# One pool of four PSUM banks for the spectral transforms and the down blocks, and filter tiles negated one step later

## The chip, the cores and the metric

The kernel runs on one core of a Trainium2 chip. Its time is device microseconds (us) of one execution; the median of three runs is given. A profile is one more execution, recorded by the hardware profiler. The engines are TensorE (PE; PEld are its weight loads), VectorE (DVE), ScalarE (ACT), GpSimd (POOL) and SyncE (SP), each with its own instruction list that it works off in order. PSUM is the accumulator memory that TensorE writes; it has eight banks of 128 x 512 fp32.

## The reference

```python
def _A_ref(x, w_r, w_i):                      # x: 1 x 2048 x 448
    X = rfft2(x, axes=(-2, -1)) * (w_r + 1j * w_i)
    return irfft2(X, s=(S, D), axes=(-2, -1))

def _B_ref(x, W_gate, W_up, W_down):          # 448 -> 1792 -> 448
    gate = x @ W_gate
    gate = gate * (gate > 0)
    return (gate * (x @ W_up)) @ W_down

xn = _layernorm(x, axis=-1)
return x + _A_ref(xn, w_r, w_i) + _B_ref(xn, W_gate, W_up, W_down)
```

So the output is the input plus a filter in the two-dimensional spectrum of the layer-normed input plus a gated MLP of the same normed input.

## The kernel before, in words

Token rows are read as 16 tiles n2 of 128 x 448 and worked on in four chunks of four tiles (512 tokens). A normed chunk stands transposed in an SBUF tile T0 to T3, as a high and a low fp16 part, so that products of three fp16 matmuls give nearly fp32 accuracy. Three kinds of work share TensorE; every one of its matmuls after the opening has the helper line L499:

- *gate/up units* (`gu_unit`): for one of the 14 slices f of the hidden width and one chunk, 20 to 22 matmuls of 128x512 into a pair of PSUM banks called gu. ScalarE then takes the relu (L1061), VectorE multiplies it by the up half (L1065, the last reader of the pair), ScalarE and VectorE split the product into its two fp16 parts h (L1069, L1073).
- *down blocks*: for one tile n2 and one group of slices (`GROUPS`, 5, 5 and 4), 15 or 12 matmuls of 128x448 into one bank called dn. A block is seeded by ScalarE with the scaled running sum xy (`dn_seed`, L1090), and ScalarE writes the bank back to xy (`dn_post`, L1101). `dn_add` (L1108) is the other way: VectorE adds a bank that was not seeded to xy; only the last four blocks (`dn_end`) use it.
- *transforms*: the forward ones `f_dft` (48 matmuls of 64x58) and `f_sdft` (fp32, 64x464) and the inverse ones `i_sdft` and `i_ddft` (48 each). Each fills two PSUM banks, the two halves of one tile fx. ScalarE empties both halves in one instruction (`f_dft` L527, `f_y` L610, `i_part` L866) or in two (`i_ddft`, L909). `two_banks` (L507) writes one element of a fresh pair by ScalarE before the first matmul; VectorE folds what f_dft gave (L538 and on, tile eb), and f_sdft reads the folded tile. `row_dft` makes two small matmuls in one bank.

PSUM is divided by tile names: gu two pairs (four banks), dn two single banks, fx one pair. In the filter stage the half-filter tiles wf come by DMA, and `wneg` (L682) negates a part of each on ScalarE.

What sets the order: the first 45 us follow a handwritten list (`OPENING`). Behind it a list of gate/up units and down blocks is walked; with each unit a share of background steps (the list `bg`, with costs by which a unit takes as many as it has room for) is emitted: LayerNorm of later chunks, folds, transforms, filter, stores. A list scheduler then puts the instructions of each engine in an order, by readiness in its own model of the engines, by priority (`high_priority`) and by constraints (`issue_after`). A different number of banks therefore also changes which instruction it finds ready, and so the order on every engine.

## Time and profile before

| what | value |
|---|---|
| median of three runs | 445.41 us (445.02 to 445.5) |
| the profiled execution | 444.57 us |
| its span (first to last instruction) | 442.8 us |
| instructions in it | 8438 |
| TensorE busy | 429.2 us, 97% |
| VectorE busy | 376.6 us, 85% |
| ScalarE busy | 261.1 us, 59% |
| mean granted TensorE clock | 0.995 |
| waits of TensorE on L499 for a semaphore, longest | 3.5 us on L507 |

A group row of the profile gives line, engine, operation, what is written and read with its size, count, busy time in all, mean of one in ns, and the engine's idle time just before them with what ended it. A timeline row gives start, length and count, with idle time before it in brackets. A row of waits gives the sum, the number and the longest. The windows give the busy time of each engine in a stretch and the granted clock of TensorE, where 1.00 is full speed.

### The profile page before, as it was taken

The page shows a single profiled execution, that of the slowest core. Times are in us where ns is not written, and L with a number is a line of the kernel's source. Part 1 is how long each engine was busy: PE and PEld are TensorE (multiplying, and loading weights), DVE is VectorE, ACT ScalarE, POOL GpSimd, SP SyncE. Part 2 cuts the span into 40 slices and gives each one's busy share as a digit, 9 for nine tenths or more (in the row PEclk, how much of TensorE's full clock was granted, in tenths as well). Part 3 has the DMA queues.
Part 4 walks back from the last instruction along what each step waited for, and adds up shares of the span by engine and source line. Part 5 has one row for each costly group of instructions (what it writes and reads, how often), then busy time and mean ns, then how long its engine had stood idle before and what let it go on. Part 6 is the DMA issues. An engine that isn't in the chain of part 4 may idle for free.

```text
span 442.8 us, 8438 instructions
## 1 busy us (share of the span) xinstructions
PE 429.2 (97%) x3222; PEld 201.6 (46%) x3222; DVE 376.6 (85%) x804; ACT 261.1 (59%) x503; POOL 29.5 (7%) x72
## 2 busy tenths in 40 slices
PE   6999999699999999999999999999999999999995
PEld 2644544344444444444444444444454544544453
DVE  6898799999386999999999999599989869869533
ACT  6897484755645674754353562675766665755752
POOL 1140040310100110000000010010000000000000
PEclk9999999999999999999999999999999999999999
DMA  7769994230000731345404000021221021230112
GB/s 257 260 155 285 333 262 51 39 72 2 2 3 6 233 104 55 96 134 151 127 19 113 1 0 1 1 57 32 49 53 43 28 71 24 71 86 0 64 64 85
DMA packets 37721, 38.63 MB, mean 87 GB/s; under 512 B 18928, under 2 KB 33072, under 8 KB 37680
## 3 DMA queue, kind: packets, MB, share of 16 engines
q1 hardware_dynamic: 37680, 38.09, 30.5%
q8 instruction: 25, 0.41, 0.4%
q14 instruction: 16, 0.13, 0.1%
HBM read 23.20 MB, written 3.67 MB: 61 GB/s over the span
## 4 chain that ended last, share of the span: by engine, by line
PE 49%; DVE 31%; DMA 8%; ACT 4%; SPq 3%; issue 3%; POOL 1%; ACTq 0%; DVEq 0%; POOLq 0%
PE gu L499 27%; PE dn L499 15%; PE fx L499 5%; DMA wst<-in_wgu 3%; DMA y<-in_xr 3%; DVE g L1065 2%; SPq L724 2%; DVE h L1073 2%; DVE y L589 2%; DVE y L590 2%; DVE y L690 2%; DVE y L691 2%; DMA sw<-y 2%; DVE y L603 1%; DVE y L602 1%
## 5 line engine op out<-in xcount | busy, mean ns | idle before, releaser
L499 PE MATMUL gu<-T,wt 128*128 128x512 f16 (+2 forms) x1250 | 269.3, 377 | 0.5 <-DVE g L1065 0.5
L499 PEld LDWEIGHTS <-wt 128*128 128x128 f16 (+1 forms) x1250 | 111.2, 98 | 145.1 <-issue 25.2
L499 PE MATMUL dn<-wdt,h 128*128 128x448 f16 x624 | 127.7, 353 | 0.1
L499 PEld LDWEIGHTS <-h 128*128 128x128 f16 x624 | 59.5, 98 | 58.3 <-issue 2.2
L1069 ACT ACTIVATE h<-g 128x512 f16<-128x512 f32 x56 | 35.1, 627 | 57.5 <-DVE g L1065 57.4
L1061 ACT ACTIVATE g<-gu 128x512 f32<-128x512 f32 x56 | 33.0, 589 | 34.6 <-PE gu L499 34.5
L1065 DVE SCALAR_TENSOR_TENSOR g<-gu,g 128x512 f32<-128x512 f32 x56 | 38.3, 685 | 17.5 <-ACT g L1061 17.4
L1073 DVE TENSOR_TENSOR h<-g,h 128x512 f16<-128x512 f32 x56 | 38.3, 686 | 8.3 <-ACT h L1069 8.1
L1101 ACT ACTIVATE xy<-dn,dsc 128x448 f32<-128x448 f32 x44 | 27.4, 627 | 25.6 <-PE dn L499 25.3
L1090 ACT ACTIVATE dn<-xy,dinv 128x448 f32<-128x448 f32 x44 | 27.5, 629 | 0.4
L961 DVE SCALAR_TENSOR_TENSOR wt<-wst,wsc,wt 128x512 f16<-128x512 f32 x28 | 20.3, 745 | 4.6 <-ACT wt L957 4.6
L957 ACT ACTIVATE wt<-wst,wsc 128x512 f16<-128x512 f32 x28 | 19.0, 711 | 1.8 <-DVE wsc L244 1.8
L237 POOL PARTITION_ALL_REDUCE wm<-wm x15 | 7.7, 515 | 174.9 <-ACT junk L234 174.9
L234 ACT ACTIVATE junk<-wst 128x512 bf16<-128x512 f32 x28 | 17.4, 622 | 3.1 <-DMA wst<-in_wgu 2.9
L909 ACT ACTIVATE xy<-fx,fsc 128x448 f32<-128x448 f32 x16 | 9.3, 631 | 15.3 <-PE fx L499 15.3
L307 DVE BATCH_NORM_STATS2 bst<-y 128x6 f32<-128x448 f32 x16 | 9.2, 615 | 6.1 <-DMA y<-in_xr 6.1
L871 DVE TENSOR_TENSOR yu<-wf 128x512 f32<-128x512 f32 x8 | 5.5, 691 | 9.1 <-ACT wf L866 9.1
L590 DVE TENSOR_TENSOR y<-y 128x928 f32<-128x928 f32 (+1 forms) x11 | 11.8, 1077 | 0.3 <-DMA row<-y 0.2
L589 DVE TENSOR_TENSOR y<-y 128x928 f32<-128x928 f32 (+1 forms) x11 | 11.9, 1077 | 0.2
L866 ACT ACTIVATE wf<-fx 128x1024 f32<-128x1024 f32 x8 | 8.1, 1018 | 5.9 <-PE fx L499 5.9
L846 DVE SCALAR_TENSOR_TENSOR vt<-wst,fsc,vt 128x464 f16<-128x464 f32 x16 | 10.5, 697 | 0.5 <-ACT vt L841 0.4
L473 DVE TENSOR_TENSOR wst<-wst 128x116 f32<-128x116 f32 x48 | 10.5, 273 | 0.2
(157 smaller groups left out, 477.7 us busy)
## 6 DMA issues: line engine op xcount, KB each, us to landing
wst<-in_wgu SPq DMA_DIRECT2D x28, 256.0 KB, 4.6
wf<-in_wf SPq DMA_DIRECT2D x16, 232.0 KB, 2.8
sw<-y SPq DMA_DIRECT2D x64, 58.0 KB, 2.0
sw<-wst SPq DMA_DIRECT2D x32, 116.0 KB, 2.2
y<-in_xr SPq DMA_DIRECT2D x16, 224.0 KB, 4.8
xy<-in_x SPq DMA_DIRECT2D x16, 224.0 KB, 4.8
out<-xy SPq DMA_DIRECT2D x15, 224.0 KB, 2.0
wdst<-in_wd SPq DMA_DIRECT2D x14, 224.0 KB, 4.5
```

Of the source, the lines that this page charges most:

```text
L234: A.activation(mt([128, 512], BF16, "junk")[:, 0:src.shape[-1]], src, AF.Square, scale=SQ, accum_out=acc)
L499: r = P.matmul(*a, **k)
L589: V.tensor_tensor(t, a, b, op=OP.add)
L590: V.tensor_tensor(b, a, b, op=OP.subtract)
L957: A.activation(w[:, 0:4, :], wst[f, g], AF.Copy, scale=wsc[f, g])
L961: V.scalar_tensor_tensor(w[:, 4:8, :], st, sc, w[:, 0:4, :], op0=OP.mult, op1=OP.subtract)
L1061: last["A"] = A.activation(g1s[f, q], hps[f, q][:, 0, :], AF.Relu, scale=2.0 ** -22).ins
L1065: last["V"] = V.scalar_tensor_tensor(g1, hps[f, q][:, 1, :], 2.0 ** -22, g1, op0=OP.mult, op1=OP.mult).ins
L1069: A.activation(ht[f, q][:, 0, :], g1s[f, q], AF.Copy)
L1073: V.tensor_tensor(h[:, 1, :], g1s.pop((f, q)), h[:, 0, :], op=OP.subtract)
L1090: A.activation(dps[n2][:, 0:D], xy[n2], AF.Copy, scale=dinv[:, g:g + 1])
L1101: last["A"] = A.activation(xy[n2], dps[n2][:, 0:D], AF.Copy, scale=dsc[:, g:g + 1]).ins
```

## The change

Transforms, down blocks, `row_dft` and the end blocks take their banks from one pool of four single banks, name dn, in turn (`dn_bank`, `fx`). A transform takes two of them. An instruction that emptied both halves of a pair is now two, one for each bank (f_dft, f_y and i_part; 24 instructions become 48). The counter `banks` counts the banks taken after the opening, and blocks that get one of the first six are *bare*: they are not seeded, their first matmul starts the sum, and `dn_post` adds them by VectorE (`dn_add`) instead of by ScalarE; three blocks are. The two matmuls of row_dft are written so that the first covers 464 columns. And `wneg` moves from the end of the step before to the head of the step that multiplies by the tile.

```diff
--- before.py
+++ after.py
@@ -172,20 +172,11 @@
         return main.tile(shape, dt, name=name, bufs=bufs)
 
     def dn_bank():
-        return psum.tile([128, 512], F32, name="dn", bufs=2)
-
-    def fx2():
-        return psum.tile([128, 2, 512], F32, name="fx", bufs=1)
+        state["banks"] = state.get("banks", 0) + ("opened" in state)
+        return psum.tile([128, 512], F32, name="dn", bufs=4)
 
     def fx():
-
-        if "opened" in state:
-            return fx2()[:, 0]
-        if "fx" not in state:
-            state["fx"] = [fx2(), 1]
-        t = state["fx"]
-        t[1] = 1 - t[1]
-        return t[0][:, t[1]]
+        return dn_bank()
 
     xv = x.rearrange("(p n) d -> p n d", n=16)
     xrv = xr.rearrange("(p n) d -> p n d", n=16)
@@ -503,9 +494,9 @@
 
     def two_banks():
 
-        t = fx2()
-        A.activation(t[:, 0, 0:1], eps, AF.Copy)
-        return t
+        banks = fx(), fx()
+        A.activation(banks[0][:, 0:1], eps, AF.Copy)
+        return banks
 
     def f_dft(a, b, m=None):
 
@@ -520,12 +511,14 @@
                     for h in (1, 0):
                         p = slice(64 * h, 64 * h + 64)
                         with tc.high_priority(offset=2000):
-                            m = chained(mm(ps[:, 1 - h, o], T[p, t, js], fd_t[p, c:c + GW], start=(k + r + i == 0),
+                            m = chained(mm(ps[1 - h][:, o], T[p, t, js], fd_t[p, c:c + GW], start=(k + r + i == 0),
                                                  stop=(i == 2), skip_group_check=True).ins, m)
         ts = fa[a] = [free.pop(0) for _ in range(2)]
-        with tc.high_priority(offset=400):
-            A.activation(joint(ts).rearrange("p n c g k -> p n (c g k)").rearrange("p n (i e) -> p n i e", i=2),
-                         ps[:, :, 0:8 * GW].rearrange("p i (n e) -> p n i e", n=2), AF.Copy, scale=2.0 ** -14)
+        o = joint(ts).rearrange("p n c g k -> p n (c g k)").rearrange("p n (i e) -> p n i e", i=2)
+        for i in range(2):
+            with tc.high_priority(offset=400):
+                A.activation(o[:, :, i], ps[i][:, 0:8 * GW].rearrange("p (n e) -> p n e", n=2), AF.Copy,
+                             scale=2.0 ** -14)
         return m
 
     def f_fold(a):
@@ -557,13 +550,13 @@
         V.tensor_tensor(Xh[n2][:, 1], f_part(a, n2), Xh[n2][:, 0], op=OP.subtract)
 
     def f_sdft(a):
-        m, w, ps = None, fm_t[a], fx2()
+        m, w, ps = None, fm_t[a], (fx(), fx())
         sfx[a] = ps
         for k in range(2):
             for b in range(2):
                 p, q = slice(64 * k, 64 * k + 64), slice(64 * b, 64 * b + 64)
                 with tc.high_priority(offset=0 if m is None else 2000):
-                    m = chained(mm(ps[q, k, 0:XW], w[p, b], f_part(a, a + 8 * b)[p], start=True, stop=True,
+                    m = chained(mm(ps[k][q, 0:XW], w[p, b], f_part(a, a + 8 * b)[p], start=True, stop=True,
                                    skip_group_check=True).ins, m)
         return m
 
@@ -606,8 +599,9 @@
 
     def f_y(a):
         yps[a] = [free.pop(0) for _ in range(2)]
-        with tc.high_priority(offset=400):
-            A.activation(joint(yps[a]).rearrange("p n c g k -> p n (c g k)"), sfx.pop(a)[:, :, 0:XW], AF.Copy)
+        for t, ps in zip(yps[a], sfx.pop(a)):
+            with tc.high_priority(offset=400):
+                A.activation(flat(t), ps[:, 0:XW], AF.Copy)
 
     def f_y1(a):
         x, y = yps.pop(a)
@@ -738,7 +732,8 @@
 
     def row_wf():
         w = state["roww"] = it([128, NG * KC], F32, "roww")
-        h = state["rowh"] = it([128, NG * KC], F16, "rowh")
+        h = state["roww2"] = it([128, XW], F16, "rowh")
+        state["rowh"] = h[:, 0:NG * KC]
         G.memset(w[0:64], 0.0)
         G.memset(w[64:128], 0.0)
         G.memset(h, 0.0)
@@ -767,9 +762,10 @@
         V.scalar_tensor_tensor(h[64:112], state["rowv"], fsc[0:48, 0:1], h[0:48], op0=OP.mult, op1=OP.subtract)
 
     def row_dft(d):
-        y = state["rowps"] = fx()[:, 0:NG * KC]
-        for a in range(2):
-            mm(y, row_t[:, d, a], state["rowh"], start=(a == 0), stop=(a == 1), skip_group_check=True)
+        ps = fx()
+        y = state["rowps"] = ps[:, 0:NG * KC]
+        for a, (o, h) in enumerate(((ps[:, 0:XW], state["roww2"]), (y, state["rowh"]))):
+            mm(o, row_t[:, d, a], h, start=(a == 0), stop=(a == 1), skip_group_check=True)
 
     def row_mul():
         y, w = state["rowps"], state["roww"]
@@ -846,7 +842,7 @@
             V.scalar_tensor_tensor(lo[:, b], u[:, b], fsc[:, 0:1], hi[:, b], op0=OP.mult, op1=OP.subtract)
 
     def i_sdft(p):
-        m, ps = None, fx2()
+        m, ps = None, (fx(), fx())
         sps[p] = ps
         for b in range(2):
             v, w = state["vt"][:, :, b].rearrange("p a g k -> p a (g k)"), im_t[p][:, b]
@@ -856,14 +852,15 @@
                     for e in range(2):
                         q = slice(64 * e, 64 * e + 64)
                         with tc.high_priority(offset=0 if m is None else 2000):
-                            m = chained(mm(ps[:, e, o], v[q, h, 128 * g:128 * (g + 1)], w[q, c],
+                            m = chained(mm(ps[e][:, o], v[q, h, 128 * g:128 * (g + 1)], w[q, c],
                                            start=(b + g + i == 0), stop=(i == 2), skip_group_check=True).ins, m)
         return m
 
     def i_part(p):
         t = state["eo"] = it([128, 2, 1024], F16, "wf", 3).bitcast(F32)
-        with tc.high_priority(offset=400):
-            A.activation(t, sps.pop(p), AF.Copy, scale=2.0 ** -14)
+        for e, ps in enumerate(sps.pop(p)):
+            with tc.high_priority(offset=400):
+                A.activation(t[:, e], ps, AF.Copy, scale=2.0 ** -14)
 
     def i_unfold(p):
         t = state["eo"]
@@ -886,8 +883,8 @@
     def i_ddft(a, b, m=None):
 
         fresh = a in seeded or b in seeded
-        banks = two_banks() if fresh else fx2()
-        sides = [banks[:, e, 0:D].rearrange("p (b d) -> p b d", b=2) for e in range(2)]
+        banks = two_banks() if fresh else (fx(), fx())
+        sides = [banks[e][:, 0:D].rearrange("p (b d) -> p b d", b=2) for e in range(2)]
         for e in range(0 if fresh else 2):
             with tc.high_priority(offset=400):
                 A.activation(sides[e], xy2[:, a, :, 224 * e:224 * (e + 1)], AF.Copy, scale=fsc[:, 2:3])
@@ -900,7 +897,7 @@
                     for e in (1, 0):
                         p = slice(64 * e, 64 * e + 64)
                         with tc.high_priority(offset=2000):
-                            m = chained(mm(banks[:, e, o], h[p, x, 128 * g:128 * (g + 1)], idc_t[p, y, c],
+                            m = chained(mm(banks[e][:, o], h[p, x, 128 * g:128 * (g + 1)], idc_t[p, y, c],
                                                  start=(fresh and k + g + i == 0), stop=(i == 2),
                                                  skip_group_check=True).ins, m)
         if not fresh:
@@ -911,7 +908,7 @@
             store(b)
             return m
         for k, n2 in enumerate((a, b)):
-            ips[n2] = [banks[:, e, 224 * k:224 * (k + 1)] for e in range(2)]
+            ips[n2] = [banks[e][:, 224 * k:224 * (k + 1)] for e in range(2)]
             if n2 in seeded:
                 late.add(n2)
             else:
@@ -1081,12 +1078,15 @@
     dps = {}
     stored = set()
 
-    seeded = set()
+    seeded, bare = set(), set()
 
     def dn_seed(g, n2):
 
         dps[n2] = dn_bank()
         seeded.add(n2)
+        if state["banks"] <= 6:
+            bare.add(n2)
+            return
         A.activation(dps[n2][:, 0:D], xy[n2], AF.Copy, scale=dinv[:, g:g + 1])
 
     def dn_mm(fs, n2):
@@ -1094,11 +1094,16 @@
         js = slice(128 * j, 128 * (j + 1))
         for f in fs:
             for a, b in ((0, 0), (0, 1), (1, 0)):
-                last["P"] = mm(dps[n2][:, 0:D], ht[f, q][:, a, js], wdt[f][:, b, :], start=False,
+                last["P"] = mm(dps[n2][:, 0:D], ht[f, q][:, a, js], wdt[f][:, b, :],
+                                     start=(n2 in bare and f == fs[0] and a + b == 0),
                                      stop=(f == fs[-1] and a == 1), skip_group_check=True).ins
 
     def dn_post(g, n2):
-        last["A"] = A.activation(xy[n2], dps[n2][:, 0:D], AF.Copy, scale=dsc[:, g:g + 1]).ins
+        if n2 in bare:
+            bare.discard(n2)
+            dn_add(g, n2, slice(0, D))
+        else:
+            last["A"] = A.activation(xy[n2], dps[n2][:, 0:D], AF.Copy, scale=dsc[:, g:g + 1]).ins
         seeded.discard(n2)
         if n2 in late:
             late.discard(n2)
@@ -1117,7 +1122,7 @@
     def dn_end(g, ns):
 
         fs = groups[g]
-        banks = [psum.tile([128, 512], F32, name="dn", bufs=2) for _ in range(2)]
+        banks = [dn_bank() for _ in range(2)]
         banks += [psum.tile([128, 2, 512], F32, name="gu", bufs=2)[:, 0] for _ in range(2)]
         banks.append(fx())
         w = [slice(0, D)] * 3 + [slice(0, D // 2), slice(D // 2, D)]
@@ -1222,6 +1227,8 @@
 
 
     for i0 in range(10):
+        for k in (ks[i0 - 2], ks[i0 - 2] + 8) if i0 > 1 else ():
+            add(0.0, wneg, k)
         if i0 < 8:
             k0 = ks[i0]
             for k in (k0, k0 + 8):
@@ -1232,8 +1239,6 @@
             add(1.2, pair, 1, *(("X", k) for k in pair_k))
         if i0 < 8:
             add(0.0, swap, *(("X", k) for k in (k0, k0 + 8)))
-        for k in (ks[i0 - 1], ks[i0 - 1] + 8) if 0 < i0 < 9 else ():
-            add(0.0, wneg, k)
         if pair_k:
             add(3.4, wmul, *pair_k)
         for k in pair_k:
```

How the instructions move on the engines is not in the diff. Three places show it; rows of the changed kernel have its own line numbers.

*TensorE, second and third gate/up unit* (before: gu_920 and gu_941, then gu_1023; after: gu_932 and gu_953, then gu_1035; dn_711, dn_716, dn_792 and dn_800 are down blocks, fx_779 and dn_785 with dn_786 the first f_sdft). Before:

```order
L499 MATMUL dn_792<-wdt_569,h_590 128x448
L499 LDWEIGHTS wt_296
L499 MATMUL gu_920<-T2_63,wt_296 128x512
L499 MATMUL fx_779<-eb_83,fm_614 64x464 x4
L499 LDWEIGHTS wt_376
L499 MATMUL gu_941<-T2_63,wt_376 128x512
```

After, from the last matmul of the third unit:

```order
L490 MATMUL gu_1035<-T2_63,wt_413 128x512
L490 MATMUL dn_785<-eb_83,fm_619 64x464 x2
L490 MATMUL dn_786<-eb_83,fm_619 64x464 x2
L490 LDWEIGHTS h_461
L490 MATMUL dn_716<-wdt_589,h_461 128x448
```

Before, two down blocks and the first f_sdft came ahead of the second unit; after, all 20 matmuls of the third unit come first, right behind those of the second, and the f_sdft and two down blocks behind it.

*VectorE, from L341 (now L332) to the first L1065 (now L1062) after it*, which frees the first of the two gu pairs (g1_976, now g1_988). Before, its last eight rows:

```order
L404 SCALAR_TENSOR_TENSOR tt1_85<-y_66,rs_905,tt1_85 128x448
L473 TENSOR_TENSOR eb_83<-eb_83 128x2x58 x2
L404 SCALAR_TENSOR_TENSOR tt2_86<-y_66,rs_905,tt2_86 128x448
L404 SCALAR_TENSOR_TENSOR tt3_87<-y_66,rs_905,tt3_87 128x448
L489 SCALAR_TENSOR_TENSOR eb_83<-eb_83 128x2x116
L490 SCALAR_TENSOR_TENSOR eb_83<-eb_83 128x2x116
L615 TENSOR_TENSOR y_66<-y_66 128x464
L1065 SCALAR_TENSOR_TENSOR g1_976<-gu_920,g1_976 128x512
```

After, its first twelve:

```order
L332 TENSOR_SCALAR rs_917<-mv_906 128x4
L322 RECIPROCAL rs_917<-rs_917 128x4
L324 SCALAR_TENSOR_TENSOR rs_917<-mv_906,rs_917 128x4
L1113 SCALAR_TENSOR_TENSOR xy_61<-dn_627,dsc_74,xy_61 128x448
L326 SCALAR_TENSOR_TENSOR rs_917<-rs_917 128x4
L328 SCALAR_TENSOR_TENSOR rs_917<-rs_917 128x4
L395 SCALAR_TENSOR_TENSOR tt0_84<-y_66,rs_917,tt0_84 128x448
L395 SCALAR_TENSOR_TENSOR tt1_85<-y_66,rs_917,tt1_85 128x448
L531 TENSOR_TENSOR eb_83<-y_66 128x16x29
L532 TENSOR_TENSOR eb_83<-y_66 128x16x29
L395 SCALAR_TENSOR_TENSOR tt2_86<-y_66,rs_917,tt2_86 128x448
L1113 SCALAR_TENSOR_TENSOR xy_61<-dn_628,dsc_74,xy_61 128x448
```

The adds of the bare blocks (L1113, dn_627 and dn_628) and the LayerNorm pieces (L395, which was L404) come early, ahead of the folds (L531 to L481); the L1062 of g1_988 stands 12 rows further on, behind the first half of the second fold and without the steps L489, L490 and L615 that came ahead of it.

*ScalarE at the first two f_dft* (fx_645 and fx_728, now dn_648 with dn_649 and dn_732 with dn_733; L388, now L379, and L390, now L381, are LayerNorm pieces). Before:

```order
L1090 ACTIVATE dn_711<-xy_61,dinv_75 128x448
L527 ACTIVATE y_66<-fx_645 128x2x464
L507 ACTIVATE fx_728<-eps_76 128x1
L1101 ACTIVATE xy_61<-dn_624,dsc_74 128x448
L324 ACTIVATE rs_905<-mv_894,eps_76 128x4
L388 ACTIVATE y_66<-y_66,rs_905 128x448
L1090 ACTIVATE dn_792<-xy_61,dinv_75 128x448
L390 ACTIVATE tt0_84<-y_66,rs_905 128x448
```

After:

```order
L315 ACTIVATE rs_917<-mv_906,eps_76 128x4
L379 ACTIVATE y_66<-y_66,rs_917 128x448 x3
L498 ACTIVATE dn_732<-eps_76 128x1
L381 ACTIVATE tt0_84<-y_66,rs_917 128x448
L381 ACTIVATE tt1_85<-y_66,rs_917 128x448
L520 ACTIVATE y_66<-dn_648 128x2x232
L520 ACTIVATE y_66<-dn_649 128x2x232
```

The seeds and posts of the down blocks are gone from here; the emptying of the first f_dft (two L520 for one L527) stands behind three LayerNorm pieces, the touch of the second pair and two more LayerNorm pieces.

## The prediction

> **What bounds the kernel now.** I read the page first, then TensorE's waits, then the places of these waits in the timelines.
>
> ```profile
> span 442.8 us, 8438 instructions
> PE 429.2 (97%) x3222; PEld 201.6 (46%) x3222; DVE 376.6 (85%) x804; ACT 261.1 (59%) x503; POOL 29.5 (7%) x72
> ```
> ```profile
> PE fx L499 <- ACT fx L507: 3.5, 1, 3.5
> ...
> PE fx L1129 <- ACT xy L909: 1.3, 1, 1.3
> ...
> PE gu L499 <- DVE g L1065: 0.5, 1, 0.5
> ```
> TensorE is busy for 429.2 of 442.8 us, so the end is TensorE's work plus its waits (us in all, times, longest). The change leaves TensorE's work as it is; it can only move waits. Three stand behind the opening: 3.5, 1.3 and 0.5 us. The first costs more than it says:
>
> ```profile
> 82.60 1.02 PE L499 MATMUL fx<-eb,fm 64*64 64x464 f32 x8
> 87.11 1.34 PE L499 MATMUL fx<-fd_t,T 64*128 64x58 f16 x48 [3.49 <-ACT fx L507]
> 88.39 5.29 PE L499 MATMUL gu<-T,wt 128*128 128x512 f16 x20
> ```
> ```profile
> 83.60:87.10 3.50, 0.02 (x3) 0.09 (x1) 3.46 (x8) 3.43 (x8) 2.02 (x5) 0.93 0.46 87
> 87.10:88.00 0.90, 0.89 (x38) 0.89 (x39) 0.90 (x3) 0.29 (x2) 0.28 (x1) 0.50 0.00 0
> 88.00:90.00 2.00, 2.00 (x23) 0.89 (x18) 2.00 (x6) 1.50 (x2) 0.00 (x0) 0.50 1.06 201
> 90.00:91.00 1.00, 1.00 (x6) 0.47 (x5) 1.00 (x4) 0.68 (x2) 0.00 (x0) 0.98 1.03 189
> ```
> In the stretches (length, busy of PE, PEld, DVE, ACT, POOL, then granted clock, DMA) the clock is 0.50 after the stall and full again at 90. The forward transform then takes 1.34 us; an undisturbed one takes 0.83 (row at 54.26 below). The 20 gate/up matmuls take 5.29; by the row at 60.83 below, 24 take 5.03, so 20 take 4.3 to 4.5. So the half clock costs 1.45 us and the stall as a whole 3.49 + 1.45 = 4.95 us. Why it stalls:
>
> ```profile
> 82.98 1.23 ACT L388 ACTIVATE y<-y,rs 128x448 f32<-128x448 f32 x2 [1.11 <-DVE eb L539]
> 84.11 1.21 ACT L390 ACTIVATE tt<-y,rs 128x448 f16<-128x448 f32 x2
> ...
> 85.93 0.92 ACT L610 ACTIVATE y<-fx 128x928 f32<-128x928 f32 x1
> 86.89 0.17 ACT L507 ACTIVATE fx<-eps 128x1 f32<-128x1 f32 x1
> ```
> The one fx pair is held by the transform of 82.60; ScalarE empties it (L610) behind LayerNorm pieces, and the touch L507 comes after that.
>
> **The change, part by part. What it takes away.** With four banks in turn the transform of 87.11 need not wait for the pair before it: -4.95 us. The 1.3 us ahead of the last down block also goes: that matmul needed the fx bank that L909 read. In the new order 24 matmuls of two other blocks stand between, 4.5 us. The 0.5 us at a gate/up unit goes because more down blocks stand ahead of that unit. Sum: -6.75 us.
>
> **What moves.** TensorE's order changes from 48 us on. These are the rows before:
>
> ```profile
> 53.03 1.30 PE L499 MATMUL dn<-wdt,h 128*128 128x448 f16 x6
> 54.26 0.83 PE L499 MATMUL fx<-fd_t,T 64*128 64x58 f16 x48
> 55.02 4.71 PE L499 MATMUL dn<-wdt,h 128*128 128x448 f16 x24
> 59.57 0.38 PE L499 MATMUL gu<-T,wt 128*128 128x512 f16 x1
> 59.88 1.02 PE L499 MATMUL fx<-eb,fm 64*64 64x464 f32 x8
> 60.83 5.03 PE L499 MATMUL gu<-T,wt 64*128 64x512 f16 x24
> 65.79 0.83 PE L499 MATMUL fx<-fd_t,T 64*128 64x58 f16 x48
> 66.56 0.82 PE L499 MATMUL gu<-T,wt 128*128 128x512 f16 x3
> ```
> The third gate/up unit (gu_1023, now gu_1035) started at 66.56. In the new order two down blocks (30 matmuls, 5.7 us by the rows), one f_sdft (1.02) and one f_dft (0.83) no longer stand ahead of it but behind: 7.5 us less. On the way there are two small new waits. The second f_dft touches its bank behind three L388 in a row and behind the VectorE add of a bare block, 0.4 us, and its later part waits until the first transform's halves are out, 0.2 us (0.2 to 1.0 together). So TensorE reaches this unit at 66.56 - 7.5 + 0.6 = 59.65.
>
> The unit has two buffers, and takes the one that L1065 of the first unit (g1_976, now g1_988) must have read. When can VectorE have done that?
>
> ```profile
> 50.59 0.17 DVE L341 TENSOR_SCALAR rs<-mv 128x4 f32<-128x4 f32 x1
> 65.32 0.68 DVE L1065 SCALAR_TENSOR_TENSOR g<-gu,g 128x512 f32<-128x512 f32 x1
> ```
> ```profile
> L1065 DVE SCALAR_TENSOR_TENSOR g<-gu,g 128x512 f32<-128x512 f32 x56 | 38.3, 685 | 17.5 <-ACT g L1061 17.4
> L473 DVE TENSOR_TENSOR eb<-eb 128x232 f32<-128x232 f32 x16 | 5.8, 405 | 0.0
> L404 DVE SCALAR_TENSOR_TENSOR tt<-y,rs,tt 128x448 f16<-128x448 f32 x8 | 5.5, 701 | 0.2 <-ACT tt L390 0.2
> L539 DVE TENSOR_TENSOR eb<-y 128x464 f32<-128x464 f32 x8 | 5.2, 655 | 0.0
> L467 DVE TENSOR_TENSOR eb<-eb 128x348 f32<-128x348 f32 x8 | 4.2, 521 | 0.2
> L473 DVE TENSOR_TENSOR eb<-eb 128x116 f32<-128x116 f32 x16 | 3.8, 279 | 0.1
> L1108 DVE SCALAR_TENSOR_TENSOR xy<-dn,dsc,xy 128x448 f32<-128x448 f32 x2 | 1.4, 684 | 0.1
> ```
> VectorE's list is unchanged up to L341, which ends at 50.76. From there to the end of that L1065 the new list has four L404, six of 128x464, two of 128x348, two of 128x232, four of 128x116, four small ones on 128x4 (by the L341 row), two L1108 and the L1065. Each starts 0.08 us before the one ahead ends: 2.5 + 3.4 + 0.9 + 0.65 + 0.8 + 0.3 + 1.2 + 0.7 = 10.45, so **61.2** without any wait. Its waits come from ScalarE:
>
> ```profile
> L388 ACT ACTIVATE y<-y,rs 128x448 f32<-128x448 f32 x8 | 5.0, 660 | 2.2 <-DVE eb L539 1.1 <-DVE y L616 0.7 <-DVE rs L341 0.3
> L527 ACT ACTIVATE y<-fx 128x928 f32<-128x928 f32 x8 | 7.4, 931 | 0.5 <-PE fx L499 0.5
> L1061 ACT ACTIVATE g<-gu 128x512 f32<-128x512 f32 x56 | 33.0, 589 | 34.6 <-PE gu L499 34.5
> L1090 ACT ACTIVATE dn<-xy,dinv 128x448 f32<-128x448 f32 x44 | 27.5, 629 | 0.4
> L909 ACT ACTIVATE xy<-fx,fsc 128x448 f32<-128x448 f32 x16 | 9.3, 631 | 15.3 <-PE fx L499 15.3
> L682 ACT ACTIVATE wf<-wf 128x116 f32<-128x116 f32 x16 | 4.3, 292 | 9.3 <-DMA wf<-in_wf 9.3
> ```
> ScalarE has three L388, a touch and an L390 (about as long as L388) from 50.8: 53.3, where L404 was ready 1.35 us before. Then one more L390 and the two halves of the first transform: 55.0, where L538 was ready 0.4 before. A half (128x464) has no row: at least half of L527, 0.47, at most L1090's 0.63; I take L1061's 0.59, the nearest size. With 0.25 for the reciprocal's ScalarE part: **63.2**. So TensorE waits 63.2 - 59.65 = **3.55 us** (bounds 1.6 and 4.0).
>
> That is as long as the old stall and I count the half clock again, **1.45 us** (0 if the wait is near its lower bound). By the Trainium skill, TensorE: Matmul & The Clock Gate, section "HAM oscillation — how this bites in real kernels", gaps over about 3.4 us are to be avoided; the clock row after the 3.49 us here agrees. By that rule a 3.55 us wait pays the 1.45 and one of 3.0 does not; the row says no more than that 3.49 was enough.
>
> **Behind it.** f_sdft (1.0), the two down blocks (5.7) and the f_dft (0.83) now follow the unit. VectorE runs dry until that f_dft is emptied: 63.2 + 4.3 + 1.45 + 7.5 = 76.45, and two halves later 77.6. From there it has 27 instructions, 10.9 us by the rows, to the fourth unit's L1065: 88.5, against TensorE's 87.65 (11.2 us of f_sdft, gate/up and f_dft): 0.8. Then 2.75 us more to the last fold step of the f_sdft that follows, which TensorE reaches after 0.9: 1.95. Together **2.75 us** (0 to 3.5). So the first 100 us change by -4.95 + 0.6 + 3.55 + 1.45 + 2.75 = +3.4.
>
> **The inverse stage.** Down blocks and inverse transforms now share banks, so a seed L1090 stands behind the emptying of the transforms. At the first down block of the last chunk group (dn_5241) TensorE has 42 matmuls of i_sdft and nine gate/up matmuls after the i_ddft, 0.7 + 1.95 = 2.65 us. ScalarE has two L909, two seeds, two halves and the seed L1090, each 0.55 after the one ahead, 3.9 us: wait **1.3**. At the second gate/up unit after the third i_sdft (gu_4977) ScalarE empties the i_sdft 2.5 us late, VectorE then needs 2.9 to that L1065, and TensorE has 22 gate/up matmuls, 4.7: wait **0.7**. Three more places between 270 and 320 us are level within 0.3 to 0.8: I count 0.8 together. Sum **2.8** (0 to 7).
>
> The filter negations (L682) move by one step; ScalarE waited 9.3 us for their tiles in all, while TensorE's three waits above are none of it, so this counts 0: it lies in ScalarE's idle time. In a stretch where ScalarE's seeds are late for TensorE the wait that goes would be a gain of a us or two, and none of the places above is one. Three bare blocks save three seeds and three posts of ScalarE (0.63 each), which lay in idle time; their VectorE adds (0.68 each) are in the sums above. The 24 split evictions add some 0.2 us each to ScalarE, which is 59% busy; where they matter they are counted.
>
> **The sum.** -6.75 + 0.6 + 3.55 + 1.45 + 2.75 + 2.8 = **+4.4 us**. The profiled execution took 444.57 (span 442.8 and 1.8 around it), 0.84 below the median of the runs; on the median: 445.41 + 4.4 = **449.8 us**.
>
> **Rivals.** (1) *Faster: VectorE is not held up.* If L404 and L538 don't wait for ScalarE, g1_988 is done at 61.2, the wait is 1.6 us, the clock stays, and of the 2.75 behind it some 1.0 is left: -6.75 + 0.6 + 1.6 + 1.0 = -3.55, and with half a microsecond in the inverse stage 442.3 us. For it: ScalarE was idle for 41% of the span. Against it: three L388 in a row stand ahead of the first transform's halves. It decides at a wait of about 3 us. (2) *No change: one stall for another.* The new wait is 3.55 but the clock stays and the inverse stage hides its waits: -6.75 + 0.6 + 3.55 + 2.75 = +0.15, 445.6 us. For it: the new list ahead of dn_5241 is the only one there with a clear lack. (3) *Slower still: the inverse stage goes in lockstep.* If each of the four inverse pairs that follow a run of down blocks costs the 1.3 us of dn_5241 and the level places lose 2.5 together, it adds 5 us: 454.8. For it: ScalarE's posts, seeds and evictions now stand in one line; against it, most gate/up work still lies between. (4) *The change doesn't do what it says:* the banks turn, but the transform of 87.11 waits as long for ScalarE's L388 and L390 ahead of its touch. Then -4.95 is not gained; I count it under (3).
>
> **The numbers.** My forecast has 0.5, rival 1 0.25, rival 2 0.12, rivals 3 and 4 0.13. What a measurement here can tell from no change is 0.2%, 0.9 us: faster is below 444.5, slower above 446.3. Faster 0.25, same 0.12, slower 0.63. The forecast's own range is 447 to 453; the range for 8 in 10 reaches to rivals 1 and 3: **442.5 to 454.5**.
>
> **What would show it.** In the new trace: no wait for the touch near 84; a wait of a gate/up unit for L1065 (now L1062) near 60 of over 3 us with a clock of 0.50 after it; VectorE idle near 70 to 77; waits of about 2 us at an f_sdft near 90; waits on ScalarE's L1090 ahead of dn_5241 near 420. If the wait near 60 is below 2 us, or VectorE reaches g1_988 before 61, the forecast's main term is wrong; if the waits after 250 us sum to more than 5, rival 3 holds.

## The result, and the profile after

The changed kernel takes **449.89 us** (median of four runs, 447.83 to 451.27) against 445.27 of the kernel before beside it (445.02 to 445.5). The ratio is 1.010, its 95% interval 1.006 to 1.014: slower by 4.6 us, where the prediction had 449.8 us and slower by 4.4. The profiled execution was the slowest of the four, 451.27 us, which is 6.7 us more than the profiled one of before. The lines of its page and its waits of TensorE that answer to those shown of before:

```profile
span 449.5 us, 8481 instructions
PE 431.8 (96%) x3222; PEld 202.8 (45%) x3222; DVE 375.3 (83%) x807; ACT 257.7 (57%) x521; POOL 30.4 (7%) x72
```
```profile
PE gu L490 <- DVE g L1062: 6.6, 6, 3.4
PE dn L490 <- issue: 2.1, 1, 2.1
...
PE dn L490 <- ACT dn L1090: 1.3, 1, 1.3
...
PE dn L490 <- ACT dn L498: 0.4, 1, 0.4
```

TensorE has the same 3222 matmuls. The span is 6.7 us longer: 2.6 us of it is busy time (431.8 against 429.2), the rest, 4.1, is idle time; behind the opening the waits over 0.1 us rose by 5.3 us (from 5.3 to 10.6), so the opening has 1.2 less. The long wait for the touch of a transform's bank (L507 before, L498 now) is 0.4 us instead of 3.5; gate/up units that wait for VectorE's L1062 (L1065 before) rose from 0.5 to 6.6 us. TensorE's timeline shows where; start, length, count, and in brackets the wait:

```profile
52.20 0.18 PE L490 MATMUL dn<-fd_t,T 64*128 64x58 f16 x1 [0.44 <-ACT dn L498]
...
62.66 5.52 PE L490 MATMUL gu<-T,wt 128*128 128x512 f16 x17 [3.42 <-DVE g L1062]
...
87.83 0.61 PE L490 MATMUL gu<-T,wt 64*128 64x512 f16 x4 [0.42 <-DVE g L1062]
...
90.50 1.69 PE L490 MATMUL dn<-eb,fm 64*64 64x464 f32 x8 [2.06 <-issue]
...
198.76 2.53 PE L490 MATMUL gu<-T,wt 128*128 128x512 f16 x11 [1.94 <-DVE g L1062]
...
427.04 1.30 PE L490 MATMUL dn<-wdt,h 128*128 128x448 f16 x6 [1.26 <-ACT dn L1090]
```

The third gate/up unit waits from 59.24 to 62.66. The clock around it, in windows that begin and end where the granted clock may change (length, busy of PE, PEld, DVE, ACT, POOL, granted clock, DMA):

```profile
59.98:63.39 3.41, 0.73 (x4) 0.38 (x4) 3.41 (x11) 1.01 (x3) 0.00 (x0) 1.00 1.22 197
63.39:66.80 3.41, 3.41 (x10) 1.19 (x9) 3.41 (x9) 0.89 (x2) 0.00 (x0) 0.50 1.17 230
...
87.28:90.70 3.42, 0.94 (x9) 0.43 (x12) 3.42 (x14) 2.88 (x7) 0.00 (x0) 1.00 0.00 0
90.70:94.11 3.41, 3.41 (x58) 1.49 (x52) 3.41 (x8) 3.41 (x8) 2.74 (x6) 0.50 0.03 7
```

In each pair the first row is the stretch with the wait, the second the stretch behind it at half clock. There are two such pairs; the prediction counted one. VectorE ran dry in between, as predicted, with 0.64 of 2.00 us busy:

```profile
68.00:70.00 2.00, 2.00 (x14) 0.62 (x13) 0.64 (x2) 0.20 (x1) 0.00 (x0) 1.00 0.02 4
```

### The profile page after: what moved, and what is told of

Same layout as the page of the kernel before. It is cut to its first block, busy times and chain, and to the rows that moved or that the text cites. A ratio compares the mean times of both kernels' runs of the same rounds, so it can differ in the third digit from the quotient of the medians.

```text
span 449.5 us, 8481 instructions
## 1 busy us (share of the span) xinstructions
PE 431.8 (96%) x3222; PEld 202.8 (45%) x3222; DVE 375.3 (83%) x807; ACT 257.7 (57%) x521; POOL 30.4 (7%) x72
## 4 chain that ended last, share of the span: by engine, by line
PE 58%; DVE 24%; DMA 6%; ACT 5%; issue 3%; SPq 3%; POOL 1%; DVEq 0%; ACTq 0%; POOLq 0%
PE gu L490 32%; PE dn L490 24%; DVE g L1062 2%; DMA y<-in_xr 2%; DVE wt L958 2%; SPq L718 2%; DVE y L583 2%; DVE bst L298 1%; DMA sw<-y 1%; PE dn L1134 1%; DVE h L1070 1%; DVE y L684 1%; DVE y L582 1%; DVE y L685 1%; DVE y L595 1%
## 5 line engine op out<-in xcount | busy, mean ns | idle before, releaser
L490 PE MATMUL gu<-T,wt 128*128 128x512 f16 (+2 forms) x1250 | 269.8, 378 | 6.6 <-DVE g L1062 6.6
L490 PEld LDWEIGHTS <-wt 128*128 128x128 f16 (+1 forms) x1250 | 111.7, 98 | 153.6 <-issue 34.4
L490 PE MATMUL dn<-wdt,h 128*128 128x448 f16 x624 | 122.7, 353 | 1.3 <-ACT dn L1090 1.3
L490 PEld LDWEIGHTS <-h 128*128 128x128 f16 x624 | 60.5, 98 | 60.1 <-issue 3.8
L1062 DVE SCALAR_TENSOR_TENSOR g<-gu,g 128x512 f32<-128x512 f32 x56 | 38.3, 683 | 5.4 <-ACT g L1058 5.4
L1106 ACT ACTIVATE xy<-dn,dsc 128x448 f32<-128x448 f32 x41 | 25.7, 628 | 25.6 <-PE dn L490 25.6
L1090 ACT ACTIVATE dn<-xy,dinv 128x448 f32<-128x448 f32 x41 | 25.2, 636 | 3.6 <-DVE row L781 3.2
L906 ACT ACTIVATE xy<-dn,fsc 128x448 f32<-128x448 f32 x16 | 9.3, 630 | 12.2 <-PE dn L490 12.2
L604 ACT ACTIVATE y<-dn 128x464 f32<-128x464 f32 x16 | 8.5, 551 | 10.1 <-PE dn L490 10.1
L837 ACT ACTIVATE vt<-wst,fsc 128x928 f16<-128x928 f32 x8 | 8.8, 1101 | 7.0 <-DVE wst L481 7.0
L490 PE MATMUL dn<-eb,fm 64*64 64x464 f32 x64 | 9.8, 620 | 2.1 <-issue 2.1
```

The source lines that it names most:

```text
L490: r = P.matmul(*a, **k)
L1062: last["V"] = V.scalar_tensor_tensor(g1, hps[f, q][:, 1, :], 2.0 ** -22, g1, op0=OP.mult, op1=OP.mult).ins
L1090: A.activation(dps[n2][:, 0:D], xy[n2], AF.Copy, scale=dinv[:, g:g + 1])
L1106: last["A"] = A.activation(xy[n2], dps[n2][:, 0:D], AF.Copy, scale=dsc[:, g:g + 1]).ins
```

## The experiments

My theory was that of the prediction: the one pool lets the transforms through, the bare blocks' adds and the new order make VectorE late for the third gate/up unit, and that wait costs its length and a stretch of half clock. The rivals: the waits behind it are the main cost; the moved `wneg` is the cause; the four banks are no gain, since splitting the evictions does the same. All times are medians, and the ratio is to the kernel before on the same chip.

| run | what it is | us | ratio (95%) |
|---|---|---|---|
| e1_again | the changed kernel once more | 449.1 | 1.0101 (1.0071 to 1.0131) |
| e2_fill8 | changed, eight idle matmuls ahead of the third unit | 444.62 | 0.9985 (0.9975 to 0.9995) |
| e3_fsdft_later | changed, transforms offered to the schedule later | 446.48 | 1.0043 (1.0026 to 1.0061) |
| e4_seeded | changed, no bare blocks | 444.54 | 1.0005 (0.9988 to 1.0023) |
| e5_before_fsdft_earlier | before, transforms offered earlier | 455.7 | 1.0232 (1.0199 to 1.0264) |
| e6_wneg_only | before, `wneg` moved | 445.27 | 1.0004 (0.9988 to 1.002) |
| e7_split_2_2 | changed, two pools of two banks, no bare blocks | 444.35 | 0.9986 (0.9968 to 1.0004) |
| e8_split_2_2_fsdft_earlier | e7, transforms offered earlier | 452.64 | 1.0163 (1.0144 to 1.0183) |
| e9_split_2_2_fwd10 | e7, only f_dft offered later | 441.11 | 0.9902 (0.9875 to 0.9929) |
| e10_bare_2_2 | e7 with the three bare blocks | 449.85 | 1.0098 (1.0065 to 1.0132) |

### The changed kernel once more

> The changed kernel once more, for the spread of its times (447.83 to 451.27 us in four runs, where the kernel before has 445.02 to 445.5). Theory: the clock gate judges stretches of 3.41 us whose boundaries lie differently in each execution, so the waits near 60 and 90 us cost a half clock in some executions and not in others; each half clock costs 1.4 us. Then the runs fall into groups by mean granted clock: about 0.992 for two half clocks (449.5 to 451.3), 0.996 for one (about 448), 1.000 for none (about 446.5). Rival: the spread comes from transfers that land at different times; then times and clocks don't go together.

Six executions gave 447.72 to 452.14 us. With the first four they fall into groups by their mean granted clock: 447.7 to 448.4 us at 0.996 (four), 449.6 to 451.3 at 0.992 (four), 451.4 and 452.1 at 0.989. One stretch of 3.41 us at half clock lowers the mean over 449.5 us by 0.0038, so these are one, two and three such stretches, each worth about 2 us. A group without any, which I had expected near 446.5 us, did not turn up. The waits were the same within 0.3 us (3.41 at the third unit, 0.42 and 2.06 near 90, 1.65 near 197). In this execution the wait at the third unit was followed by two stretches of half clock, not one:

```profile
57.38:60.79 3.41, 1.18 (x6) 0.42 (x5) 3.41 (x9) 1.63 (x4) 0.52 (x2) 1.00 1.14 258
60.79:64.21 3.42, 2.24 (x6) 0.86 (x6) 3.42 (x10) 1.64 (x3) 0.00 (x0) 0.50 1.19 246
64.21:67.62 3.41, 3.41 (x10) 1.21 (x9) 3.34 (x12) 0.00 (x0) 0.00 (x0) 0.50 0.32 60
67.62:71.03 3.41, 3.41 (x21) 1.21 (x20) 0.33 (x2) 0.80 (x3) 0.00 (x0) 1.00 0.01 2
```

So the spread of 4.4 us of one and the same program goes, for the most part, with the number of these stretches. That they fall on the same two places in each execution is shown only for the two that were profiled.

### Eight idle matmuls ahead of the third unit

They multiply a tile of zeros at the end of the second gate/up unit, so that TensorE is busy for part of the wait. Nothing is left out of the computation.

```diff
-            gu_full(f, q, gs, cs, False, True)
+            fill = 8 if (f, q) == (2, CHUNKS[1]) else 0
+            gu_full(f, q, (0,), cs, False, True)
+            gu_full(f, q, (1,), cs, False, not fill)
+            for i in range(fill):
+                last["P"] = mm(hps[f, q][:, 1, cs], state["zero"], Tq[q][:, 0, cs], start=False,
+                               stop=(i == fill - 1)).ins
```

> The changed kernel with eight more 128x512 matmuls by a tile of zeros at the end of the second gate/up unit, so that TensorE works for 1.7 us of the 3.4 us that it waits near 60. Nothing else should change its time there, since the third unit waits for VectorE anyway; the scheduler also moves the f_sdft and some of the third unit. Theory (the half clock follows from little work in a stretch): no half clock near 63, so 1.4 us less than the changed kernel in executions where that has one: about 448.4 us. Rival (the gate doesn't see such a filling, or the half clock has another cause): 449.9 or, if the fillers delay the second unit's relu, 450.5.

It took 444.62 us, 3.8 us less than expected. The wait that was left:

```profile
58.59 1.89 PE L490 MATMUL gu<-T,zero 128*128 128x512 f16 x8
...
61.24 2.75 PE L490 MATMUL gu<-T,wt 128*128 128x512 f16 x12 [0.76 <-DVE g L1067]
```

The idle matmuls filled 1.89 us, the wait fell to 0.76, and the clock there stayed at 1.00. But the scheduler also put the f_sdft in the middle of the third unit and moved what stands behind it, so the 2.06 and 0.42 us near 90 and the second half clock went too. The run shows that the half clock goes when TensorE is kept busy; how much of the 5 us that is worth it does not show, since the order is another.

### Transforms offered later

`offer` is the helper by which a background step that needs TensorE is put into the list; its constant says how many us later in the model the transform stands.

```diff
-        state["job"] = (state["at"], fn, a, 6.0)
+        state["job"] = (state["at"], fn, a, 12.0)
```

> The changed kernel with the look-ahead for transforms at 12 instead of 6 us, by which the f_sdft near 89 us comes after the 20 matmuls of the fourth gate/up unit. Theory: its wait of 2.06 us for VectorE's last fold step is covered by 4.3 us of matmuls, and with it the half clock after 90 us goes: 2.06 + 1.4 = 3.5 us less, about 446.4 us. Rival (the wait moves to the next unit that needs VectorE, gu_1534 or gu_1555): less than 1 us gained, 449 us or more.

446.48 us, as expected. The f_sdft near 90 no longer waits:

```profile
92.24 1.02 PE L490 MATMUL dn<-eb,fm 64*64 64x464 f32 x8
```

The 3.41 us at the third unit stayed (58.73 to 62.15), with one stretch of half clock after it. So about 3 of the 4.6 us go with this edit (2.6 against e1, on the same chip): the wait of 2.06 us, the half clock behind it, and part of the wait near 197, which fell to 0.94 as well.

### No bare blocks

Each of the first banks is opened by one matmul, and the block is then seeded by ScalarE and emptied by ScalarE as before the change. The opening matmul's product is written over by the seed.

```diff
         if state["banks"] <= 6:
-            bare.add(n2)
-            return
+            mm(dps[n2], Tq[CHUNKS[0]][:, 0, 0:128], Tq[CHUNKS[0]][:, 1, :], start=True, stop=True)
```

> The changed kernel with no bare blocks: all blocks are seeded and written back by ScalarE as before, and one more matmul of 128x512 on each of the first banks (its result is overwritten by the seed) stands ahead of the seed. Theory (the early VectorE adds and the order of the down blocks that comes with bare blocks make VectorE late for the third gate/up unit): in this order down blocks and the first f_sdft stand ahead of that unit again; the wait near 60 (3.42 us), its half clock (1.4) and the waits behind (2.5 and a half clock) go, a wait of about 1.2 at the fifth f_sdft comes; about 444 us. Rival (four shared banks as such delay VectorE, by the emptying of the first f_dft behind ScalarE's LayerNorm pieces): a wait of over 2 us near 60 stays, 448 us or more.

444.54 us, the time of before (ratio 1.0005). There is no wait near 60; fifteen matmuls of a down block stand there without a gap before them, and the third unit follows at 67.37:

```profile
60.99 3.00 PE L490 MATMUL dn<-wdt,h 128*128 128x448 f16 x15
```

In its place TensorE waits 0.99 us at 86 and 1.61 at 102. Six executions at a clock of 1.000 took 444.2 to 444.7, four at 0.996 took 446.4 to 447.1. So in the one pool the third unit waits only with the bare blocks and the order that comes with them; without them the pool of four made no difference that can be measured. In e4 VectorE ends L1062 earlier, at 58.35, and TensorE comes to the third unit later, at 67.37, so this run doesn't tell which of the two counts; e10 below does.

### Before, transforms offered earlier

This was to take the old 3.49 us away by order alone, with the banks as they were.

```diff
-        state["job"] = (state["at"], fn, a, 6.0)
+        state["job"] = (state["at"], fn, a, 4.0)
```

> The kernel before, with the look-ahead for transforms at 4 instead of 6 us and nothing else: the f_sdft ahead of the old stall comes 16 gate/up matmuls (3.4 us) earlier, so ScalarE empties its banks before the LayerNorm pieces and TensorE doesn't wait near 84. Theory (the old stall cost 3.49 us and a half clock; what the changed kernel set out to remove could be had without sharing banks): no half clock, mean clock 1.000, about 441 us. Rival (the wait moves to the fourth unit, whose L1065 VectorE then reaches level with TensorE, or to the next f_sdft): 444 us or more.

455.7 us: the expectation failed. The 3.49 us wait near 84 went, but the touch L507 is now late at two other places, by 2.89 us at 72 and by 2.47 at 123. And the same constant governs the inverse transforms, which now stand ahead of what they need:

```profile
349.09 0.27 PE L499 MATMUL fx<-idc_t,wf 64*128 64x56 f16 x4 [4.48 <-ACT wf L878]
352.12 1.21 PE L499 MATMUL fx<-idc_t,wf 64*128 64x56 f16 x44 [2.76 <-DVE wf L882]
```

With half clock after each of the three places, that is the 11 us: the waits behind the opening sum to 14.1 us against 5.3, and four stretches are at half clock against one.

### Only the negation moved

```diff
     for i0 in range(10):
+        for k in (ks[i0 - 2], ks[i0 - 2] + 8) if i0 > 1 else ():
+            add(0.0, wneg, k)
...
-        for k in (ks[i0 - 1], ks[i0 - 1] + 8) if 0 < i0 < 9 else ():
-            add(0.0, wneg, k)
```

> The kernel before with the second part of the change alone: the filter tiles are negated at the head of the step that multiplies them. Theory: ScalarE's waits for these tiles (9.3 us) go and TensorE's time stays, 445.3 us within 0.5; TensorE's waits of 3.5, 1.3 and 0.5 us stay. Rival (a ScalarE that no longer waits is earlier with what VectorE needs between 145 and 280 us): the 0.5 us wait near 245 goes and the time is 0.5 to 1 us shorter.

445.27 us, ratio 1.0004 (0.9988 to 1.002). The waits of TensorE of before are all there, the last one a little larger:

```profile
PE fx L499 <- ACT fx L507: 3.5, 1, 3.5
PE fx L1129 <- ACT xy L909: 1.4, 1, 1.4
PE gu L499 <- DVE g L1065: 1.1, 2, 0.8
```

ScalarE's waits for the tiles fell from 9.3 to 3.7 us, where I had expected them to go. This part of the change costs and brings nothing that can be measured in the time.

### Two pools of two banks

The evictions stay split and the transforms take single banks, but two pools of two stand in place of the one of four, with no bare blocks.

```diff
     def dn_bank():
         return psum.tile([128, 512], F32, name="dn", bufs=2)
...
     def fx():
+        return psum.tile([128, 512], F32, name="fx", bufs=2)
```

> The changed kernel with its four banks as two pools of two, one for down blocks and one for transforms, so that they are not shared; evictions split by bank; no bare blocks (the banks are the same kinds as before). Theory (sharing and bare blocks changed the order of work; splitting the evictions alone does nothing): TensorE's order near 60 is that of the kernel before, the old wait near 84 stays at 3 to 3.6 us with its half clock, 445.3 us within 0.8. Rival (half a pair that is freed early is what helps): the wait near 84 is below 2 us and the time below 443.

444.35 us, a ratio whose interval includes 1. The wait at the old place is there, but 1.94 and 0.29 us, not the 3 to 3.6 that I had expected; the first half of the rival came true, its time below 443 did not:

```profile
85.03 0.18 PE L489 MATMUL fx<-fd_t,T 64*128 64x58 f16 x1 [1.94 <-ACT fx L497]
85.51 0.81 PE L489 MATMUL fx<-fd_t,T 64*128 64x58 f16 x47 [0.29 <-ACT y L603]
```
```profile
84.06 0.54 ACT L603 ACTIVATE y<-fx 128x464 f32<-128x464 f32 x1
84.83 0.16 ACT L497 ACTIVATE fx<-eps 128x1 f32<-128x1 f32 x1
84.92 0.54 ACT L603 ACTIVATE y<-fx 128x464 f32<-128x464 f32 x1
```

The touch (L497) now stands behind the first half of the eviction (L603) and not behind both. The 1.3 us at the last down block went too. Three executions at a clock of 1.000 took 443.07 to 443.13 us, seven at 0.996 had a median of 444.6: the same program loses 1.5 us with one stretch of half clock. Presumably it follows the wait of 1.9 us when that falls so; the profiled execution is one of those at 1.000 and doesn't show it.

### The same, offered earlier

```diff
-        state["job"] = (state["at"], fn, a, 6.0)
+        state["job"] = (state["at"], fn, a, 4.0)
```

> The two pools of two banks with the look-ahead at 4 us. Theory: as in the kernel before with that look-ahead the f_sdft comes earlier and the old stall goes, and the split evictions neither add nor save: about 441 us, no half clock. Rival: the f_sdft now stands ahead of what VectorE must have folded for it and TensorE waits there, 443 us or more.

452.64 us, where 441 was expected: as in e5, the inverse transforms waited (4.62 us at 340, 2.16 at 345, half clock from 343 to 353). Splitting the evictions does not help against that.

### Only the forward transform offered later

```diff
-        state["job"] = (state["at"], fn, a, 6.0)
+        state["job"] = (state["at"], fn, a, 10.0 if fn is f_dft else 6.0)
```

> The two pools of two banks with the look-ahead at 10 us for the forward transforms alone (the inverse keep 6): 19 matmuls of the fourth gate/up unit now stand between the f_sdft and the f_dft that waited near 84, and the next pair comes 3 us later. Theory: the 1.94 us wait and, in the executions that have it, the half clock (1.5 us between the two groups of the two-pool kernel) go: 441.5 us, mean clock 1.000 in all executions. Rival (VectorE gets the next fold later and a later f_sdft or the filter stage waits for it): 443 us or more.

**441.11 us** (440.58 to 441.46), ratio 0.9902 (0.9875 to 0.9929): as expected, and better than both kernels. The clock was at least 0.999 in every execution. Its timeline at the old place:

```profile
82.44 1.02 PE L489 MATMUL fx<-eb,fm 64*64 64x464 f32 x8
83.39 4.27 PE L489 MATMUL gu<-T,wt 128*128 128x512 f16 x19
87.59 0.20 PE L489 MATMUL fx<-fd_t,T 64*128 64x58 f16 x1
```

Nineteen gate/up matmuls, 4.27 us, stand between the f_sdft and the f_dft that needs its banks. With two transform banks, emptied one by one, the stall goes when other work stands between. Whether this order alone, in the kernel before, does as much was not tried.

### Bare blocks without the one pool

```diff
     def dn_seed(g, n2):
...
+        if state["banks"] <= 3:
+            bare.add(n2)
+            return
```

> The two pools of two banks, not shared, with three bare blocks as in the changed kernel: their VectorE adds are there, ahead of L1065 of the first unit. TensorE's order near 60 has two down blocks ahead of the third unit. Theory (the wait near 60 came from the order, in which the third unit overtook two down blocks and the f_sdft; the VectorE adds alone, 1.2 us, stay inside the cover of the down blocks): no wait above 1 us near 60, about 445 us. Rival (the adds on a full VectorE are what costs): a wait of 1.5 us or more near 60 to 66 and 446.5 us or more.

No wait over 1 us near 60, as expected, but 449.85 us in place of 445. VectorE frees the gu pair even later than in the changed kernel, at 65.62 us against 62.61, and yet TensorE hardly waits for it:

```profile
64.93 0.69 DVE L1062 SCALAR_TENSOR_TENSOR g<-gu,g 128x512 f32<-128x512 f32 x1
```
```profile
65.67 1.46 PE L490 MATMUL gu<-T,wt 128*128 128x512 f16 x6 [0.20 <-DVE g L1062]
```

Two down blocks and an f_sdft stand ahead of this matmul, so TensorE comes to it at 65.47 and not at 59.24. A late VectorE alone thus makes no wait near 60; it takes the changed kernel's order on TensorE, by which the third unit comes 6 us earlier. The cost stands at the old place:

```profile
89.25 1.34 PE L490 MATMUL fx<-fd_t,T 64*128 64x58 f16 x48 [4.38 <-ACT fx L498]
```
```profile
88.01 0.98 ACT L604 ACTIVATE y<-fx 128x464 f32<-128x464 f32 x2
89.03 0.17 ACT L498 ACTIVATE fx<-eps 128x1 f32<-128x1 f32 x1
```

ScalarE comes later to the eviction than in e7 (the touch 4.2 us later, at 89.03 against 84.83), and the clock is half from 85.95 to 92.78. The three bare blocks, with the order that the scheduler makes of them, are the only difference from e7, so they cost here 5.5 us against it (5.0 by the two ratios, since the chips differ). That the way goes over VectorE, which has three adds more and for which ScalarE then waits, is argued, not shown by a run of its own.

## Why the prediction was right, point by point

**What was taken away.** The three waits of before went, as the prediction says. Their price, 6.75 us, is borne out in part: e9 has none of the three, 0.33, 0.61, 0.24 and 0.16 us of its own and no half clock, so it should stand 5.4 us below before, and stands 4.3 below (medians). Where the rest is lost is not shown. The groups of TensorE, of before and of after, seem to point at the i_sdft, 8.8 us in after (8.5 in e7 and e9) against 7.2:

```profile
L499 PE MATMUL fx<-im,vt 64*128 64x64 f16 x384 | 7.2, 190 | 0.0
```
```profile
L490 PE MATMUL dn<-im,vt 64*128 64x64 f16 x384 | 8.8, 190 | 0.0
```

One matmul lasts as long (190 ns) in both, but now the first ones of most transforms stand by themselves among other matmuls. A group's time counts such a matmul in full, though the next matmul begins before it ends (in e9 at 391.18, for 0.20 us, with the next at 391.31). Counted in the traces from each start to the next, the 384 matmuls take 6.6 us before, 6.7 after and 7.5 in e9. So this is up to 0.9 us of e9's loss, and next to nothing in the changed kernel.

**The third gate/up unit.** Predicted: reached at 59.65, held to 63.2 for 3.55 us. Measured: 59.24, 62.66 and 3.42. VectorE's rows on the way:

```profile
50.10 0.17 DVE L332 TENSOR_SCALAR rs<-mv 128x4 f32<-128x4 f32 x1
...
52.77 1.39 DVE L395 SCALAR_TENSOR_TENSOR tt<-y,rs,tt 128x448 f16<-128x448 f32 x2 [1.09 <-ACT tt L381]
...
54.22 0.64 DVE L531 TENSOR_TENSOR eb<-y 128x464 f32<-128x464 f32 x1
...
61.93 0.68 DVE L1062 SCALAR_TENSOR_TENSOR g<-gu,g 128x512 f32<-128x512 f32 x1
```

The list began at 50.10 and not at 50.59. The wait of L395 (L404 before) for ScalarE was 1.09 us where 1.35 was predicted. The 0.4 us for the two halves is not there: L531 follows at once. A half took 0.55 us, where I took 0.59:

```profile
L520 ACT ACTIVATE y<-dn 128x464 f32<-128x464 f32 x16 | 7.9, 548 | 2.1 <-PE dn L490 2.1
```

From the end of L332 to the end of L1062 VectorE took 12.34 us; the prediction has 12.44 from L341 on. Two errors cancel in it: VectorE waited 1.25 us for ScalarE (1.09 and 0.16) and not 2.0, and its instructions took 0.6 us more than the 10.45. So the path held, and part of the close match in its size is luck. That the path needs both arrivals is shown by two runs: in e4, without the bare blocks, the wait is gone; in e10 VectorE is later still, but TensorE comes later too, and 0.20 us is left. Rival 1 falls here; it needed a VectorE that is not held up by ScalarE.

**The touch** cost 0.44 us, against 0.6 for touch and halves.

**The half clock.** One stretch follows the 3.42 us, as predicted (two in the profiled execution of e1). The price of 1.45 us took 4.3 to 4.5 us for 20 full-speed matmuls; the row that it names (24 in 5.03) gives 4.2, so 1.6. A stretch cost 1.5 us by the groups of e7 and 2.3 by those of e4. What was wrong is the count. The wait of 2.06 us for f_sdft was priced at its length alone; with the 0.42 us before it in the same stretch it brought a second half clock, which the sum has not. By the Trainium skill, TensorE: Matmul & The Clock Gate, section "HAM oscillation — how this bites in real kernels", gaps over about 3.4 us are to be avoided; here a gap of 2.06 us and one of 0.42 in a stretch of 3.41 were enough, and the measurement decides. Not every gap is enough: the 1.94 us near 197 were followed by full clock. Rival 2, in which the clock stays, falls.

**Behind it.** Predicted 0.8 + 1.95 us near 88 (1.85 by its own 2.75 less 0.9); measured 0.42 and 2.06.

**The inverse stage.** dn_5241 waits 1.26 us, as predicted (1.3). The place of gu_4977 has two waits, 0.26 and 0.23, where 0.7 was predicted; the level places cost 0.33 and 0.27 (near 269 and 299) where I counted 0.8:

```profile
268.63 13.75 PE L490 MATMUL gu<-T,wt 128*128 128x512 f16 x64 [0.33 <-DVE g L1062]
```

Sum 2.35 against 2.8, and rival 3, five us more, falls. So does rival 4: the touch near 84 is not late any more.

**The negation** counted nothing: e6 says the same.

**What the sum had not.** A wait of 1.94 us at a gate/up unit near 197, a place that the prediction doesn't mention. VectorE comes to it without a gap:

```profile
196.28 1.27 DVE L991 SCALAR_TENSOR_TENSOR wdt<-wdst,wds,wdt 128x448 f16<-128x448 f32 x2
197.48 0.63 DVE L595 SCALAR_TENSOR_TENSOR y<-y 128x464 f32<-128x464 f32 x1
198.03 0.68 DVE L1062 SCALAR_TENSOR_TENSOR g<-gu,g 128x512 f32<-128x512 f32 x1
```

A wait of 0.94 to 1.65 us stands there (190 to 199) in e1, e2, e3 and e4 too, and in none of e7, e9 and e10; so it comes with the one pool's order and not with the bare blocks. Which of the instructions that moved makes VectorE late was not tried.

The measured terms add up: -6.75 + 0.44 + 3.42 + 1.45 + 2.48 + 2.35 + 1.94 = +5.3. To the +6.7 of the profiled execution 1.4 is left: 2.6 more of busy time and 1.2 less of waits in the opening. Of the 2.6, one more stretch of half clock explains 1.5 to 2.3; the rest I did not trace. The median of the four is 1.4 us below that execution. The half clock doesn't explain it, since the two executions around the median had the same mean clock, 0.992.

So the total of +4.4 came nearer to the median's +4.6 than its parts did: a wait of 1.94 us and a stretch of half clock are missing from the sum, 1.0 us of the waits in it is too much, the opening gave 1.2 that were not forecast, and the executions differ by 3.4 us. The forecast's mechanism and its main term held; that the total came within 0.2 us is luck. The step that fell short is "I count the half clock again, **1.45 us**", which is right for the third unit and leaves out the second place, 25 us on. What the parts are in an execution with one such stretch stays open, since none of those was profiled.

## What to carry to other kernels

When buffers are shared, the wait for the buffer goes, but the order of every engine moves with it: list what each engine does from the place of change to the next reader of the scarce buffer, and compare the arrival times, as the third unit shows. Before buying a stall away with more buffers, look whether other work can stand between the two users: here one constant in the order, on top of the split banks, made the kernel 4.3 us faster than before (e9; the split banks alone, e7, changed the time by less than the runs tell), and the four banks gained nothing (e4). And price a stall of the matmul engine by the stretch it lies in: two short ones close together, here 0.42 and 2.06 us, can cost as much clock as one long.

## What the runs showed of the hardware that I had not expected

The clock is granted in stretches of 3.41 us, with other bounds in each execution. Whether half clock follows doesn't go by the length of one gap: in e10 the clock fell 1.07 us into a gap (84.88 to 85.95), and near 197 a gap of 1.94 us left it full. It goes, but only roughly, by the busy time within the stretch. Rows of e10, e7 and the changed kernel show it:

```profile
82.53:85.95 3.42, 1.90 (x12) 0.48 (x9) 3.13 (x8) 2.67 (x6) 1.51 (x3) 1.00 0.02 5
85.95:89.37 3.42, 0.12 (x6) 0.12 (x7) 3.39 (x8) 3.25 (x9) 2.38 (x6) 0.50 0.46 88
```
```profile
81.22:84.64 3.42, 1.88 (x14) 0.41 (x13) 3.39 (x7) 3.38 (x7) 2.70 (x6) 1.00 0.24 47
84.64:88.05 3.41, 2.73 (x57) 1.64 (x57) 3.41 (x10) 2.17 (x7) 1.40 (x4) 1.00 0.60 113
```
```profile
196.51:199.92 3.41, 1.47 (x8) 0.60 (x7) 3.41 (x7) 1.18 (x3) 0.00 (x0) 1.00 0.72 224
199.92:203.34 3.42, 3.42 (x18) 1.41 (x18) 3.42 (x6) 2.04 (x7) 0.00 (x0) 1.00 0.37 89
```

In the traces of all twelve kernels, behind the opening, each stretch at full clock with at most 1.21 us busy was followed by half clock, and each with at least 1.93 was not. Between them the busy time doesn't decide: 1.90 us (e10) lost the clock, while 1.47 (the changed kernel, the wait of 1.94 us near 197), 1.85 (e1) and 1.88 (e7) kept it. In e10 the eight matmuls of f_sdft count as 1.45 us, against 1.02 in e7; with 1.02 that stretch would have 1.47 too. What is counted, and where the limit lies, stays open.

Back to full the way is longer: in e1 a stretch of 2.24 us busy at half clock (60.79 to 64.21) was followed by another at half clock, and so was one of 2.69 in e8; 2.92 us, in the kernel before (86.62 to 90.03), were followed by full clock. A stretch costs 1.5 us by the two groups of e7 and about 2.3 by those of e4 (444.3 and 446.6). So the same program can have several times, as e7, e4 and the changed kernel do. In e9, without such waits, the mean clock was 0.999 or 1.000 in all six executions, and they lie within 0.9 us.
